# First layer of a three-layer kernel: the transposes of kv move to the bank of kv's sum and ahead of those of q; the second step of the unit loop gets an order of its own

## The chip, the cores and the metric

One Trainium2 chip, one of its cores. The metric is the device time of the program in microseconds (us). The kernel before takes 558.27 us, the median of three runs (557.97 to 558.54). TensorE is called PE here, VectorE DVE, ScalarE ACT, GpSimd POOL, and SP is the engine that issues the DMAs.

## The reference

Three layers follow one another: linear attention, a layer of four attention experts, a layer of eight feed-forward experts. The change is in the first alone. With 4 batches, 8 heads, 576 positions, 64 dimensions and 128 features:

```
def phi(x):                                   # x: q or k, [b, h, s, d]
    proj = x @ w_phi                          # [64, 128]
    proj = proj - max(abs(proj), axis=-1)     # per position
    return concat([exp(proj), exp(-proj)])    # 256 features
q_p, k_p = phi(q), phi(k)
kv  = einsum('bhsf,bhsd->bhfd', k_p, v)
z   = sum(k_p, axis=s)
out = (q_p @ kv) / (q_p . z + 1e-6)
```

The second layer takes out, the third takes the second's result; all of it is fp32.

## The kernel before, in words

The class PhaseA computes the first layer. A unit is one batch and one pair of heads, so there are 16 units. For each unit:

- proj (lines 221 to 243) projects k (512 positions, "k"), q (512 positions, "q") and the last 64 positions of both together ("e"). For k and q two PSUM tiles, one for each head (pjk, pjq), hold the product; DVE takes the largest absolute value (mxk, line 241) and subtracts it (uk, line 242).
- feat_k (line 245) takes the exponentials of uk and ue with both signs on ACT into a_kp, of which there is one buffer (lines 251 and 252), and POOL sums them towards z (zs, lines 255 to 257).
- feat_q (line 259) transposes uq on PE, one head at a time (tile tr, line 268), and ACT takes the exponentials into qp (line 270).
- kv (line 272) accumulates kv on PE in a PSUM tile Y (line 279, 20 rows of the profile for a unit); keys (line 282) adds the sums z to the same tile (line 288), and ACT copies it to kvt (line 291).
- kvtrans (line 293) transposes ue of one unit (line 301) and kvt of the unit before it (line 306) on PE into one PSUM tile, also called kvt in the profile. ACT copies kvt's part to kvs (line 307) and takes exponentials of ue's part into the last 64 columns of qp (line 311).
- num (line 313) and den (line 330) multiply qp by kvs: the tiles pn and, every second unit, pd.

PSUM has eight banks. The pool of the first layer gives five of them to the tags X and tr together (class Banks, and ps.same = {"tr": ("X", 5), "X": ("X", 5)}), two to mm (pje, pn, pd) and one to Y. A unit takes seven tiles of the five: pjk twice, pjq twice, tr twice, and kvtrans' tile. A tile's first matmul waits until the last reader of the bank's earlier tile is done.

run (line 379) goes over 18 steps i: it projects unit i, makes features, kv and z of unit i-1, and num and den of unit i-2. The order of what each step emits is the string A_STEPS: "k0 e0 q0" are projections, "t" gives work of the later layers its turn, "f0", "f1" are feat_q by head, "x0" is kvtrans, "kv0" to "kv3" the sum, "n0 n1" num, "z0" feat_k, "s0" keys, "d0 d1" den. A scheduler then orders what is ready on each engine; each engine runs its list strictly in order. Constants (an identity matrix, counters and the like) are made by make_consts before all this, in part on DVE.

```
A_STEPS = ("k0 e0 q0 t f0 x0 t f1 t a kv0 kv1 A t kv2 kv3 t n0 n1 z0 a t t A s0 d0 d1 t")
pt = self.ps.tile([128, 512], F32, tag="X", name=f"kvt_{i}_{j}")                # kvtrans
r["Y"] = ps.tile([128, 512], F32, tag="Y", name=f"Y_{i}", bufs=1)               # feat_q, h == 0
```

Of the kernel before, what the change touches and what calls it, by code (L numbers as in the profile page):

```python
# [20 lines left out]
NF = 128  # L21
# [11 lines left out]

A_STEPS = ("k0 e0 q0 t f0 x0 t f1 t a kv0 kv1 A t kv2 kv3 t n0 n1 z0 a t t A s0 d0 d1 t")

# [105 lines left out]
def make_consts(ctx, tc, E1=4, E2=8):  # L145
    nc = tc.nc
    cp = ctx.enter_context(tc.tile_pool(name="consts", bufs=1))
    k = Consts()
    one = cp.tile([128, 128], F32, name="ones")
    make_identity(nc, one)  # L150
    eye = cp.tile([128, 128], F32R, name="ident")
    nc.vector.tensor_copy(eye, one)
    k.ident = rd(eye)
    k.identb = cp.tile([128, 128], BF16, name="identb")
    nc.vector.tensor_copy(k.identb, k.ident)
    k.mask = cp.tile([128, 128], BF16, name="cmask")
# [12 lines left out]
    nc.vector.tensor_copy(k.iota, ii)
    k.iota1 = cp.tile([128, 8], F32, name="iota1")  # L170
    nc.vector.tensor_scalar(k.iota1, k.iota, 1.0, None, op0=OP.add)

    k.lower = cp.tile([128, 4, 4], F32, name="lower")
    nc.vector.tensor_tensor(k.lower, k.iota[:, None, 0:4].to_broadcast([128, 4, 4]),
                            k.iota[:, 0:4, None].to_broadcast([128, 4, 4]), op=OP.is_lt)
    return k


class PhaseA:


    def __init__(self, ctx, tc, k, ps, gk, dr, hl, kq, v, w_phi, x1_tile, bg):
        nc = tc.nc
        self.gk, self.dr, self.hl = gk, dr, hl
        self.nc, self.k, self.kq, self.v, self.bg, self.x1_tile = nc, k, kq, v, bg, x1_tile
        self.p2 = ctx.enter_context(tc.tile_pool(name="a_2", bufs=2))
        self.p3 = ctx.enter_context(tc.tile_pool(name="a_3", bufs=2))
        self.p1 = ctx.enter_context(tc.tile_pool(name="a_1", bufs=2))
        self.ps = ps
        self.w_phi = self.p3.tile([128, NF], F32, name="a_w", bufs=1)  # L190
        self.w_in = w_phi
        self.vts = []
# [28 lines left out]
    def proj(self, i, nm):  # L221


        nc, r = self.nc, self.st[i]
        w, raws = self.w_phi, r["raw"]
        n = 1 if nm == "e" else 4
        u = r["u" + nm] = self.p3.tile([128, n, 256], F32, tag=f"u{nm}", name=f"u{nm}_{i}")
        mx = self.p3.tile([128, 2, n], F32, tag=f"mx{nm}", name=f"mx{nm}_{i}")
        if n == 1:
            pt = [self.ps.tile([128, HALF], F32, tag="mm", name=f"pj{nm}_{i}_{h}") for h in range(2)]  # L230
        else:
            pt = [self.ps.tile([128, 512], F32, tag="X", name=f"pj{nm}_{i}_{h}") for h in range(2)]
        for t in range(n):
            for h in range(2):
                p = slice(64 * h, 64 * h + 64)
                c = dict(k=0, e=512, q=640)[nm] + 128 * t
                nc.tensor.matmul(pt[h][:, 128 * t:128 * t + 128], raws[p, c:c + 128], w[p], start=True, stop=True)  # L237
        for h in range(2):
            src = pt[h][:, 0:128 * n].rearrange("p (t f) -> p t f", f=NF)
            m = mx[:, h]  # L240
            nc.vector.tensor_reduce(m, src, axis=AX.X, op=OP.max, apply_absolute_value=True)  # L241
            self.bg.anchor(nc.vector.tensor_tensor(u[:, :, NF * h:NF * h + NF], src,  # L242
                                                   m[:, :, None].to_broadcast([128, n, NF]), op=OP.subtract))

    def feat_k(self, i):
        nc, r = self.nc, self.st[i]
        u, e = r["uk"], r["ue"]
        kp = self.kp
        zs = r["zs"] = self.p3.tile([128, 2, 2, 256], F32, tag="zs", name=f"zs_{i}", bufs=1)
        for sg, sc in ((0, 1.0), (1, -1.0)):  # L250
            nc.scalar.activation(kp[:, 0:4, sg, :], u[:, 0:4, :], AF.Exp, scale=sc)  # L251
            self.bg.anchor(nc.scalar.activation(kp[0:64, 4, sg, :], e[0:64, 0, :], AF.Exp, scale=sc))

            add = nc.gpsimd.tensor_tensor
            add(zs[:, :, sg, :], kp[:, 0:2, sg, :], kp[:, 2:4, sg, :], op=OP.add)  # L255
            add(zs[0:64, 0, sg, :], zs[0:64, 0, sg, :], kp[0:64, 4, sg, :], op=OP.add)
            add(zs[:, 0, sg, :], zs[:, 0, sg, :], zs[:, 1, sg, :], op=OP.add)

    def feat_q(self, i, h):
        nc, r, ps, k = self.nc, self.st[i], self.ps, self.k  # L260
        u = r["uq"]
        if h == 0:
            r["qp"] = self.p1.tile([128, 2, 2, S], F32, tag="qp", name=f"qp_{i}", bufs=3)
            r["Y"] = ps.tile([128, 512], F32, tag="Y", name=f"Y_{i}", bufs=1)
        qp = r["qp"]
        tp = ps.tile([128, 512], F32, tag="tr", name=f"tr_{i}_{h}")
        for t in range(4):
# [4 lines left out]
    def kv(self, i, n):  # L272

        nc, r, k = self.nc, self.st[i], self.k
        Y = r["Y"]
        vt, kp = r["v"], self.kp
        for t in ((0, 1), (2,), (3,), (4,))[n]:
            for h in range(2):
                nc.tensor.matmul(Y[64 * h:64 * h + 64, 0:256], vt[:, t, h, :],  # L279
                                 kp[:, t, :, h * NF:(h + 1) * NF], start=t == 0, stop=t == 4)  # L280

    def keys(self, i):
        nc, r, k = self.nc, self.st[i], self.k
# [95 lines left out]
    def run(self, batch_done, after):  # L379
# [5 lines left out]
        for i in range(n + 2):  # L385
# [1346 lines left out]
```

## Time and profile before

| | us |
|---|---|
| median of three runs | 558.27 |
| the profiled execution | 558.66 |
| its span in the profile | 556.9 |
| PE busy | 530.4 (95%) |
| DVE busy | 364.8 (66%) |
| ACT busy | 264.8 (48%) |
| POOL busy | 148.3 (27%) |

The profiled execution is 1.76 us longer than its span, which is time around the first and the last instruction. Times in rows are counted from the span's start. The first layer takes about the first 180 us, in which work of the second layer is mixed in from about 85 us on. Matmul records are pipelined, so that their durations overlap; a distance from one start to the next is the better measure of what a group costs.

### The profile page before, as it was taken

Reading aid. Unit: us, or ns where it says so; the run is one execution under the profiler, and the core shown is the slowest. Engines: PE = TensorE matmul, PEld = TensorE weight load, DVE = VectorE, ACT = ScalarE, POOL = GpSimd, SP = SyncE. Lnnn points to the kernel's source line nnn. Section 1 sums busy time; section 2 is a strip of 40 time slices with the busy share of each in tenths; the row PEclk is TensorE's granted clock in tenths of the full one; section 3 lists DMA queues with packets and bytes.
Section 4 is the critical chain, followed back from the end, with each engine's and each line's share of the span. In section 5 each row is a group of like instructions: output and inputs, shape, how many; then the busy total and the mean of one; then the engine's idle time right before and its main releaser. Section 6 shows DMA issues by size and latency. Waiting matters only on the chain.

```text
span 556.9 us, 11719 instructions
## 1 busy us (share of the span) xinstructions
PE 530.4 (95%) x4456; PEld 440.7 (79%) x4456; DVE 364.8 (66%) x970; ACT 264.8 (48%) x601; POOL 148.3 (27%) x212
## 2 busy tenths in 40 slices
PE   7999999899999999998999999999999999999995
PEld 6666665566666597767767798999999999999995
DVE  5776677986772777878897776863656274717440
ACT  2857465574474466857656553530434044305200
POOL 5563594368537232020244400000000000000000
PEclk9999999999999999999999999999999999999999
DMA  8323263444105221700200420254435133623011
GB/s 246 124 76 119 79 229 105 123 145 160 61 5 153 96 69 47 254 16 1 78 1 1 140 88 2 77 180 150 144 114 193 46 124 114 234 88 124 2 45 47
DMA packets 32707, 57.05 MB, mean 102 GB/s; under 512 B 7012, under 2 KB 17636, under 8 KB 31620
## 3 DMA queue, kind: packets, MB, share of 16 engines
q1 hardware_dynamic: 32644, 56.24, 31.0%
q8 instruction: 37, 0.61, 0.4%
q14 instruction: 26, 0.21, 0.1%
HBM read 41.86 MB, written 14.36 MB: 101 GB/s over the span
## 4 chain that ended last, share of the span: by engine, by line
PE 75%; DVE 16%; ACT 3%; issue 2%; DMA 2%; SPq 0%; POOL 0%; DVEq 0%; ACTq 0%
PE po_c L63 6%; PE po_c L64 6%; PE po_c L65 6%; PE Y L279 6%; PE ph_c L63 5%; PE ph_c L65 5%; PE ph_c L64 5%; PE pn L323 5%; PE pq_s L702 4%; PE pd L340 3%; PE py_s L848 3%; PE pjk L237 3%; DVE mxk L241 3%; DVE uk L242 2%; PE pt_s L821 2%
## 5 line engine op out<-in xcount | busy, mean ns | idle before, releaser
L63 PE MATMUL ph_c<-xh_c,w1h_c 128*128 128x288 f32 x256 | 76.8, 301 | 0.0
L63 PE MATMUL po_c<-h_c,w2h_c 128*128 128x288 f32 x256 | 76.3, 298 | 0.0
L1415 ACT ACTIVATE h_c<-ph_c 128x288 fp32r<-128x288 f32 x64 | 26.0, 409 | 105.1 <-PE ph_c L65 104.8
L64 PE MATMUL ph_c<-xl_c,w1h_c 128*128 128x288 f32 x256 | 75.8, 296 | 0.0
L64 PE MATMUL po_c<-h_c,w2h_c 128*128 128x288 f32 x256 | 75.6, 295 | 0.0
L65 PE MATMUL ph_c<-xh_c,w1l_c 128*128 128x288 f32 x256 | 75.6, 296 | 0.0
L65 PE MATMUL po_c<-h_c,w2l_c 128*128 128x288 f32 x256 | 75.5, 295 | 0.0
L255 POOL TENSOR_TENSOR zs<-a_kp 128x512 f32<-128x512 f32 x32 | 42.2, 1336 | 69.2 <-PE Y L288 42.7
L270 ACT ACTIVATE qp<-tr 128x512 f32<-128x512 f32 x64 | 35.1, 610 | 50.2 <-PE tr L268 50.2
L1416 DVE SCALAR_TENSOR_TENSOR h_c<-ph_c,h_c 128x288 fp32r<-128x288 f32 x64 | 28.9, 454 | 33.8 <-ACT h_c L1415 33.2
L63 PEld LDWEIGHTS ph_c<-xh_c,w1h_c 128*128 128x128 f32 x256 | 48.1, 188 | 1.7 <-issue 0.9
L63 PEld LDWEIGHTS po_c<-h_c,w2h_c 128*128 128x128 f32 x256 | 48.2, 188 | 0.9 <-issue 0.9
L65 PEld LDWEIGHTS ph_c<-xh_c,w1l_c 128*128 128x128 f32 x256 | 48.1, 188 | 0.5 <-issue 0.5
L64 PEld LDWEIGHTS ph_c<-xl_c,w1h_c 128*128 128x128 f32 x256 | 48.2, 188 | 0.0
L65 PEld LDWEIGHTS po_c<-h_c,w2l_c 128*128 128x128 f32 x256 | 48.2, 188 | 0.0
L64 PEld LDWEIGHTS po_c<-h_c,w2h_c 128*128 128x128 f32 x256 | 48.1, 188 | 0.0
L702 PE MATMUL pq_s<-xh_b,w_s 128*128 128x288 f32 x192 | 43.5, 305 | 1.7 <-DVE q_s L670 1.7
L1438 DVE TENSOR_TENSOR fo_c<-po_c,pb 128x288 f32<-128x288 f32 x32 | 14.5, 455 | 44.5 <-PE po_c L65 44.5
L279 PE MATMUL Y<-a_kp,a_v 128*64 128x256 f32 x320 | 41.1, 386 | 0.0
L251 ACT ACTIVATE a_kp<-uk 128x1024 f32<-128x1024 f32 x32 | 33.6, 1052 | 13.0 <-DVE uk L242 6.4
L323 PE MATMUL pn<-qp,kvs 128*64 128x288 f32 x256 | 36.1, 408 | 0.0
L702 PEld LDWEIGHTS pq_s<-xh_b,w_s 128*128 128x128 f32 x192 | 31.9, 188 | 4.1 <-issue 2.3
(314 smaller groups left out, 1218.9 us busy)
## 6 DMA issues: line engine op xcount, KB each, us to landing
w1raw_c<-in_w_dram SPq DMA_DIRECT2D x16, 512.0 KB, 4.2
w2raw_c<-in_w_dram SPq DMA_DIRECT2D x16, 512.0 KB, 4.4
raw<-in_kq_dram SPq DMA_DIRECT2D x15, 320.0 KB, 3.1
rb<-d SPq DMA_DIRECT2D x32, 144.0 KB, 3.2
x1d<-x SPq DMA_DIRECT2D x4, 1152.0 KB
x2d<-x SPq DMA_DIRECT2D x4, 1152.0 KB
raw<-in_kq_dram SPq DMA_DIRECT2D x16, 256.0 KB, 3.3
a_v<-in_v_dram SPq DMA_DIRECT2D x16, 256.0 KB, 4.2
```

The costliest lines, as they stand in the source:

```text
L63: nc.tensor.matmul(out, lh, rh, start=start, stop=False, **kw)
L64: nc.tensor.matmul(out, lh, rl, start=False, stop=False, **kw)
L65: return nc.tensor.matmul(out, ll, rh, start=False, stop=stop, **kw)
L237: nc.tensor.matmul(pt[h][:, 128 * t:128 * t + 128], raws[p, c:c + 128], w[p], start=True, stop=True)
L251: nc.scalar.activation(kp[:, 0:4, sg, :], u[:, 0:4, :], AF.Exp, scale=sc)
L255: add(zs[:, :, sg, :], kp[:, 0:2, sg, :], kp[:, 2:4, sg, :], op=OP.add)
L270: self.bg.anchor(nc.scalar.activation(qp[:, h, sg, 0:512], tp, AF.Exp, scale=sc))
L279: nc.tensor.matmul(Y[64 * h:64 * h + 64, 0:256], vt[:, t, h, :], kp[:, t, :, h * NF:(h + 1) * NF], start=t == 0, stop=t == 4)
L323: nc.tensor.matmul(pn[64 * h:64 * h + 64, :], kvs[:, sg, 64 * h:64 * h + 64], qp[:, h, sg, c], start=sg == 0, stop=sg == 1)
L702: self.nc.tensor.matmul(out, self.wqkv[t][:, wj, ch, 0:m], x[:, ch, c], start=wj == ch == 0 and x is xh, stop=wj == 1 and ch == 3)
L1415: nc.scalar.activation(hh[:, c], ph, AF.Relu),
L1416: nc.vector.scalar_tensor_tensor(hl[:, c], ph, 0.0, rd(hh[:, c]), op0=OP.max, op1=OP.subtract))
```

## The change

Three things are edited, all in the first layer.

- kvtrans takes its tile from the tag Y (one bank) and no longer from X, and A_STEPS has x0 ahead of f0. The tiles qp and Y are now allocated in kvtrans and kv.
- Step i = 1 has its own order, A_STEPS_1: behind the second unit's k come x0 and the whole kv of the first unit, and only then the second unit's e and q; its matmuls are told to be issued behind the last matmul of that kv.
- In the beginning, each pair "largest value, difference" of the first unit, and of the second unit's k, is issued behind the one before it, the first behind the last constant; and the exponentials of the first unit's k are taken by head, four of 512 columns for two of 1024.

```diff
-A_STEPS = ("k0 e0 q0 t f0 x0 t f1 t a kv0 kv1 A t kv2 kv3 t n0 n1 z0 a t t A s0 d0 d1 t")
+A_STEPS = ("k0 e0 q0 t x0 f0 t f1 t a kv0 kv1 A t kv2 kv3 t n0 n1 z0 a t t A s0 d0 d1 t")
+A_STEPS_1 = ("k0 t x0 kv0 kv1 t kv2 kv3 e0 q0 t f0 t f1 t z0 t t s0 t")
...
+                with ExitStack() as x:
+                    if i == 1 and nm != "k":
+                        x.enter_context(after(self.kv_last.ins))
+                    nc.tensor.matmul(pt[h][:, 128 * t:128 * t + 128], raws[p, c:c + 128], w[p], start=True, stop=True)
...
+            with ExitStack() as x:
+                if i == 0 or i == 1 and nm == "k":
+                    x.enter_context(after(self.last.ins))
+                nc.vector.tensor_reduce(m, src, axis=AX.X, op=OP.max, apply_absolute_value=True)
+            last = nc.vector.tensor_tensor(u[:, :, NF * h:NF * h + NF], src,
+                                           m[:, :, None].to_broadcast([128, n, NF]), op=OP.subtract)
+            self.last = last
...
+        if not i:
+            for h in range(2):
+                for sg, sc in ((0, 1.0), (1, -1.0)):
+                    c = slice(h * NF, (h + 1) * NF)
+                    nc.scalar.activation(kp[:, 0:4, sg, c], u[:, 0:4, c], AF.Exp, scale=sc)
...
-        if h == 0:
-            r["qp"] = self.p1.tile([128, 2, 2, S], F32, tag="qp", name=f"qp_{i}", bufs=3)
-            r["Y"] = ps.tile([128, 512], F32, tag="Y", name=f"Y_{i}", bufs=1)
...
+        if n == 0:
+            r["Y"] = self.ps.tile([128, 512], F32, tag="Y", name=f"Y_{i}", bufs=1)
...
-        pt = self.ps.tile([128, 512], F32, tag="X", name=f"kvt_{i}_{j}")
+        pt = self.ps.tile([128, 512], F32, tag="Y", name=f"kvt_{i}_{j}", bufs=1)
         if j >= 0:
             r = self.st[j]
+            r["qp"] = self.p1.tile([128, 2, 2, S], F32, tag="qp", name=f"qp_{j}", bufs=3)
...
-            for step in A_STEPS.split():
+            for step in (A_STEPS_1 if i == 1 else A_STEPS).split():
```

First place: PE in the middle of a usual step, before. tr_0 and tr_1 are q's transposes by head, kvt_2 kvtrans' tile, Y the sum; in brackets stands what a row waits for.

```order
L268 MATMUL tr_0_471<-ident,uq_339 128x128 x4
L301 MATMUL kvt_2_478<-ident,ue_329 128x128 [waits DVE_49,PE_49]
L301 MATMUL kvt_2_478<-ident,ue_329 128x128
L306 MATMUL kvt_2_478<-ident,kvt_420 128x128 [waits Activation_49]
L306 MATMUL kvt_2_478<-ident,kvt_420 128x128 x2
L268 MATMUL tr_1_488<-ident,uq_339 128x128 [waits DVE_49,PE_49]
L268 MATMUL tr_1_488<-ident,uq_339 128x128 x3
L279 MATMUL Y_470<-a_kp,a_v_139 64x256 [waits DMAHW0_49]
L279 MATMUL Y_470<-a_kp,a_v_139 64x256 x7
```

The same step of the changed kernel on PE:

```order
L317 MATMUL kvt_2_471<-ident,ue_331 128x128 [waits Activation_49]
L317 MATMUL kvt_2_471<-ident,ue_331 128x128
L322 MATMUL kvt_2_471<-ident,kvt_422 128x128 x3
L281 MATMUL tr_0_482<-ident,uq_341 128x128 x4
L281 MATMUL tr_1_489<-ident,uq_341 128x128 [waits DVE_49,PE_49]
L281 MATMUL tr_1_489<-ident,uq_341 128x128 x3
L294 MATMUL Y_496<-a_kp,a_v_139 64x256 [waits DMAHW0_49,PE_49,Activation_49]
L294 MATMUL Y_496<-a_kp,a_v_139 64x256 x7
```

kvt now stands first and waits for ACT alone; the second head's transposes still wait for DVE; and Y's first matmul waits for ACT as well.

Second place: ACT in the first two units, before (uk_158 and ue_174 are the first unit's, uk_218 and ue_234 the second's).

```order
L251 ACTIVATE a_kp<-uk_158 128x4x256 x2
L252 ACTIVATE a_kp<-ue_174 64x256 x2
L270 ACTIVATE qp_260<-tr_0_262 128x512 x2
L311 ACTIVATE qp_260<-kvt_-1_0_269 128x2x64 x2
L251 ACTIVATE a_kp<-uk_218 128x4x256
L270 ACTIVATE qp_260<-tr_1_274 128x512 x2
L252 ACTIVATE a_kp<-ue_234 64x256
L251 ACTIVATE a_kp<-uk_218 128x4x256
L252 ACTIVATE a_kp<-ue_234 64x256
L291 ACTIVATE kvt_306<-Y_261 128x384
```

The same of the changed kernel (there uk_220 and ue_253 are the second unit's):

```order
L264 ACTIVATE a_kp<-uk_158 128x4x128 x4
L268 ACTIVATE a_kp<-ue_174 64x256 x2
L327 ACTIVATE qp_237<-kvt_-1_0_236 128x2x64 x2
L267 ACTIVATE a_kp<-uk_220 128x4x256 x2
L283 ACTIVATE qp_237<-tr_0_279 128x512 x2
L283 ACTIVATE qp_237<-tr_1_286 128x512 x2
L268 ACTIVATE a_kp<-ue_253 64x256 x2
L306 ACTIVATE kvt_308<-Y_242 128x384
```

Both exponentials of the second unit's k now stand ahead of all those of the first unit's q, and the copy of Y stays behind them.

Third place: DVE in the beginning, before, from the first projection to the first difference of e.

```order
L241 TENSOR_REDUCE mxk_159<-pjk_0_160 128x4
L241 TENSOR_REDUCE mxk_159<-pjk_1_161 128x4
L242 TENSOR_TENSOR uk_158<-pjk_0_160,mxk_159 128x4x128
L242 TENSOR_TENSOR uk_158<-pjk_1_161,mxk_159 128x4x128
L169 CAST iota<-iota_i 128x8
L241 TENSOR_REDUCE mxe_175<-pje_0_176 128x1
L152 CAST ident<-ones 128x128
L163 CAST cmaskr<-cmask 128x64
L171 TENSOR_SCALAR iota_79<-iota 128x8
L155 CAST identb<-ident 128x128
L165 MEMSET ones 128x128
```

The same of the changed kernel, from the last constants on:

```order
L166 MEMSET ones 128x128
L175 TENSOR_TENSOR lower<-iota 128x16
L1027 COPY b_ex<-iota 128x8
L249 TENSOR_REDUCE mxk_159<-pjk_0_160 128x4
L250 TENSOR_TENSOR uk_158<-pjk_0_160,mxk_159 128x4x128
L249 TENSOR_REDUCE mxk_159<-pjk_1_161 128x4
L250 TENSOR_TENSOR uk_158<-pjk_1_161,mxk_159 128x4x128
L249 TENSOR_REDUCE mxe_175<-pje_0_176 128x1
L250 TENSOR_TENSOR ue_174<-pje_0_176,mxe_175 128x128
```

All constants come ahead of the first projection's values, and each difference stands right behind its own largest value.

## Rows read from the trace of the kernel before

**Rows 1.** The page, the chain that ended last, shares of the span by engine.
```profile
PE 75%; DVE 16%; ACT 3%; issue 2%; DMA 2%; SPq 0%; POOL 0%; DVEq 0%; ACTq 0%
```
**Rows 2.** Waits of PE, 0 to 180 us: total us, times, longest.
```profile
PE kvt L301 <- DVE uk L242: 4.6, 11, 1.0
```
**Rows 3.** Timeline of a usual unit: start us, us, instruction, idle before.
```profile
39.95 0.66 PE L268 MATMUL tr<-ident,uq 128*128 128x128 f32 x4
40.14 1.28 DVE L242 TENSOR_TENSOR uk<-pjk,mxk 128x512 f32<-128x512 f32 x2
...
40.96 0.41 PE L301 MATMUL kvt<-ident,ue 128*128 128x128 f32 x2 [0.36 <-DVE uk L242]
...
41.21 0.49 PE L306 MATMUL kvt<-ident,kvt 128*128 128x128 f32 x3
...
41.56 0.63 PE L268 MATMUL tr<-ident,uq 128*128 128x128 f32 x4
...
41.74 0.49 ACT L307 ACTIVATE kvs<-kvt 128x384 f32<-128x384 f32 x1
...
42.12 2.38 PE L279 MATMUL Y<-a_kp,a_v 128*64 128x256 f32 x20
42.12 0.44 ACT L311 ACTIVATE qp<-kvt 128x128 f32<-128x128 f32 x2
...
46.73 1.16 PE L237 MATMUL pjk<-a_w,raw 64*128 64x128 f32 x16
```
**Rows 4.** Timeline of the first 27 us.
```profile
5.87 1.29 DVE L241 TENSOR_REDUCE mxk<-pjk 128x4 f32<-128x512 f32 x2 [4.94 <-PE pjk L237]
...
9.42 0.28 DVE L241 TENSOR_REDUCE mxe<-pje 128x1 f32<-128x128 f32 x1
...
15.40 0.46 ACT L311 ACTIVATE qp<-kvt_-1_0_269 128x128 f32<-128x128 f32 x2
...
15.72 1.08 ACT L251 ACTIVATE a_kp<-uk 128x1024 f32<-128x1024 f32 x1
...
15.98 0.66 PE L268 MATMUL tr<-ident,uq 128*128 128x128 f32 x4
...
16.68 1.10 ACT L270 ACTIVATE qp<-tr 128x512 f32<-128x512 f32 x2
...
17.65 0.41 ACT L252 ACTIVATE a_kp<-ue 64x256 f32<-64x256 f32 x1
...
17.95 1.05 ACT L251 ACTIVATE a_kp<-uk 128x1024 f32<-128x1024 f32 x1
...
19.21 0.47 ACT L291 ACTIVATE kvt<-Y 128x384 f32<-128x384 f32 x1
...
26.58 1.16 PE L237 MATMUL pjk<-a_w,raw 64*128 64x128 f32 x16
```
**Rows 5.** Timeline of DVE, a difference right behind its own largest value.
```profile
95.55 0.67 DVE L241 TENSOR_REDUCE mxq<-pjq 128x4 f32<-128x512 f32 x1
96.25 0.69 DVE L242 TENSOR_TENSOR uq<-pjq,mxq 128x512 f32<-128x512 f32 x1
```
**Rows 6.** Timeline of PE, the units whose wait is not the usual one.
```profile
118.96 0.41 PE L301 MATMUL kvt<-ident,ue 128*128 128x128 f32 x2 [0.48 <-DVE uk L242]
129.74 0.41 PE L301 MATMUL kvt<-ident,ue 128*128 128x128 f32 x2 [0.16 <-DVE uk L242]
139.92 0.63 PE L268 MATMUL tr<-ident,uq 128*128 128x128 f32 x4 [0.36 <-DVE uk L242]
```
**Rows 7.** Busy us by stretch: length, PE, PEld, DVE, ACT, POOL, clock, DMA.
```profile
100.00:120.00 20.00, 18.32 (x185) 12.09 (x184) 19.00 (x50) 11.28 (x24) 9.26 (x10) 1.00 0.43 127
```
**Rows 8.** Timeline of POOL and DVE near 90 us.
```profile
89.05 2.55 POOL L255 TENSOR_TENSOR zs<-a_kp 128x512 f32<-128x512 f32 x2 [4.53 <-PE Y L288]
...
90.28 1.36 DVE L483 TENSOR_TENSOR w<-L,mx 128x20 f32<-128x20 f32 x1
```
**Rows 9.** Line 483, 80 to 300 us: duration ns min/median/max.
```profile
L483 DVE TENSOR_TENSOR w<-L,mx x4: 171/172/1360, 90.3 to 250.2; 128x20 f32<-128x20 f32 x4
```

More of the change, by code (lines that the diff above doesn't have):

```diff
@@ L173, in make_consts @@
     k.lower = cp.tile([128, 4, 4], F32, name="lower")
-    nc.vector.tensor_tensor(k.lower, k.iota[:, None, 0:4].to_broadcast([128, 4, 4]),
-                            k.iota[:, 0:4, None].to_broadcast([128, 4, 4]), op=OP.is_lt)
+    k.last = nc.vector.tensor_tensor(k.lower, k.iota[:, None, 0:4].to_broadcast([128, 4, 4]),
+                                     k.iota[:, 0:4, None].to_broadcast([128, 4, 4]), op=OP.is_lt)
     return k
@@ L199, in __init__ @@
         nc.gpsimd.memset(self.kp[64:128, 4], 0.0)
+        self.last = k.last
         self.st = {}
@@ L221, in proj @@
     def proj(self, i, nm):
-        nc, r = self.nc, self.st[i]
+        nc, r, after = self.nc, self.st[i], self.bg.tc.issue_after
         w, raws = self.w_phi, r["raw"]
@@ L236, in proj @@
                 c = dict(k=0, e=512, q=640)[nm] + 128 * t
-                nc.tensor.matmul(pt[h][:, 128 * t:128 * t + 128], raws[p, c:c + 128], w[p], start=True, stop=True)
+                with ExitStack() as x:
+                    if i == 1 and nm != "k":
+                        x.enter_context(after(self.kv_last.ins))
+                    nc.tensor.matmul(pt[h][:, 128 * t:128 * t + 128], raws[p, c:c + 128], w[p], start=True, stop=True)
         for h in range(2):
@@ L240, in proj @@
             m = mx[:, h]
-            nc.vector.tensor_reduce(m, src, axis=AX.X, op=OP.max, apply_absolute_value=True)
-            self.bg.anchor(nc.vector.tensor_tensor(u[:, :, NF * h:NF * h + NF], src,
-                                                   m[:, :, None].to_broadcast([128, n, NF]), op=OP.subtract))
+            with ExitStack() as x:
[5 more added lines that the diff above has]
+            self.last = last
+            self.bg.anchor(last)
     def feat_k(self, i):
@@ L249, in feat_k @@
         zs = r["zs"] = self.p3.tile([128, 2, 2, 256], F32, tag="zs", name=f"zs_{i}", bufs=1)
+        if not i:
[3 more added lines that the diff above has]
+                    nc.scalar.activation(kp[:, 0:4, sg, c], u[:, 0:4, c], AF.Exp, scale=sc)
         for sg, sc in ((0, 1.0), (1, -1.0)):
-            nc.scalar.activation(kp[:, 0:4, sg, :], u[:, 0:4, :], AF.Exp, scale=sc)
+            if i:
+                nc.scalar.activation(kp[:, 0:4, sg, :], u[:, 0:4, :], AF.Exp, scale=sc)
             self.bg.anchor(nc.scalar.activation(kp[0:64, 4, sg, :], e[0:64, 0, :], AF.Exp, scale=sc))
@@ L278, in kv @@
             for h in range(2):
-                nc.tensor.matmul(Y[64 * h:64 * h + 64, 0:256], vt[:, t, h, :],
-                                 kp[:, t, :, h * NF:(h + 1) * NF], start=t == 0, stop=t == 4)
+                self.kv_last = nc.tensor.matmul(Y[64 * h:64 * h + 64, 0:256], vt[:, t, h, :],
+                                                kp[:, t, :, h * NF:(h + 1) * NF], start=t == 0, stop=t == 4)
     def keys(self, i):
```

## The prediction

> **What bounds the kernel now.** I read the page first, then PE's waits over the first layer, then the timeline of one usual unit, then that of the first 27 us, and last the stretch in which the second layer's gate is computed beside the first. The chain that ended last runs on PE for 75% of the span and on DVE for 16% [rows 1], so time is won where PE waits, and where DVE is the chain. In the first 180 us one wait of PE comes back: line 301 waits for the difference uk, 11 times, 4.6 us in all [rows 2].
>
> The timeline of a usual unit shows what this wait is. q's first transposes start at 39.95; then PE stands idle for 0.36 us until DVE has written uk's first half, and goes on with kvtrans at 40.96 [rows 3]. The data has nothing to do with uk: kvtrans transposes ue and kvt, both of units before. It is the bank. A unit takes seven tiles of five banks, and the sixth, kvtrans', falls on that of the same unit's pjk, which DVE still reads. The Trainium skill says the same of such a picture (Perfetto Trace Analysis, Optimization Strategy: a gap that comes back at the same place on the engine that should be busy can mean too few buffers in PSUM); the sum doesn't rest on it.
>
> **The change, usual units.** Measured from start to start, kvtrans takes 41.56 − 40.96 = 0.60 us, four transposes of q 42.12 − 41.56 = 0.56, and from Y's start to the next unit's k it is 46.73 − 42.12 = 4.61 [rows 3]. Before, from q's first transposes to Y it is 42.12 − 39.95 = 2.17. After, kvtrans is first, with a bank that ACT has left long before, and six tiles remain for the five banks, so the one that meets pjk's bank is q's second transposes. 0.60 + 0.56 + 0.56 = 1.72, so 0.45 are to be had (the 0.36 of idle time, and the pipeline's running empty). Two waits can eat of it:
>
> - The second transposes of q wait for uk's first half. It lands at 40.14 + 0.68 = 40.82 (half of 1.28 and an overlap of 0.08), PE went on 0.14 behind that; after the change they would be due at 39.95 + 0.60 + 0.56 = 41.11 [rows 3]. Nothing to wait for.
> - Y now shares its bank with kvtrans' tile, so its first matmul waits until ACT has read that tile: the copy to kvs, and two exponentials. ACT's copy starts 41.74 − 40.96 = 0.78 behind kvtrans' start, and the last exponential ends at 42.12 + 0.44 = 42.56, 1.60 behind it [rows 3]. PE starts behind such a release at 15.98, where the exponentials ended at 15.40 + 0.46 = 15.86: 0.12 more [rows 4]. That makes 1.72, exactly when PE is through with its 1.72 of transposes. So there is no cover left: whatever ACT is late, Y is late.
>
> What stands behind Y on PE is num, keys and the next unit's k, so a late Y delays all. The bounds of a usual unit: 0.45 if ACT keeps these times, and 0.15 if the three reads don't overlap as they do here (an estimate: 0.49 and twice some 0.30, 0.30 us longer). I take 0.40, near the upper end, because the times of ACT are rows of these very instructions. Eight units are usual: six up to 82 us and two near 153 and 162 us; of the 4.6 us, less the long one and the two below, each has (4.6 − 1.0 − 0.48 − 0.16) / 8 = 0.37 [rows 2, 6], as the one shown. 8 × 0.40 = 3.2 us.
>
> **The other units.** At 93.58, the longest of the 11, DVE is the bound and not PE: DVE is busy for 19.00 of 20 us between 100 and 120 us [rows 7], and PE's waits there give nothing. At 118.96 [rows 6] PE had put six matmuls of Y ahead of the wait, which now come behind it, 6 × 0.12 = 0.7 us (2.38 us for 20 [rows 3]) against 0.60 for kvtrans, which moves ahead: 0. At 129.74 the wait is 0.16 [rows 6], so 0.2. At 139.92 q's transposes themselves wait [rows 6], since the gate's transposes take a bank too; kvtrans now fills that gap: 0.4, with 0 as the other end, for Y then waits for ACT in a busier place. Together 0.6.
>
> **The beginning.** Here the chain is DVE and then ACT. Constants go where DVE waited for the first k (4.94 us idle before 5.87 [rows 4]), so they cost nothing. But each difference now stands right behind its own largest value, and 95.55 to 96.25 shows the price of that: 0.70 from start to start [rows 5], for 0.60 where another instruction stands between. DVE after the change: first unit's k, from 5.87 [rows 4], 0.70 + 0.60 + 0.70 + 0.60 = 2.6, to 8.47; four short ones of e (0.28 each [rows 4], an estimate of 0.25 apart), to 9.47; q 2.6, to 12.07; the second unit's k with one short one between, 0.70 + 0.60 + 0.60 + 0.20 + 0.68, to 14.85.
>
> ACT has the first unit's exponentials done, and the first Y ends, well before this: uk's first head is there at 7.25; four exponentials of 0.54 with a gap between the heads end near 9.7, e's and kvtrans' at some 10.7, and 20 matmuls of 0.12 end near 13.2. So the four exponentials for two, and the early Y, are covered by 1.6 us, and become the chain only if these take that much longer. From 14.85 on ACT is the chain, in its new order: two exponentials of uk, 2 × 0.96 (15.72 to 16.68); two pairs for q, 2 × 0.97 (16.68 to 17.65); two of ue, 2 × 0.30 (17.65 to 17.95); the copy of Y, 0.47 [rows 4]. With 0.03 for the first start that is 19.81, and PE starts the third step's kvtrans at 19.93. With 1.72 to Y and 4.61 to the next k it is 26.26, where before it is 26.58 [rows 4]: 0.3 us won. Most of what the early Y gives is lost again at ACT, where the copy of Y stands behind eight other instructions. The bounds: 1.3, if the copy is not held up and PE goes on without a stop (the third unit's q needs banks that DVE leaves, with three short ones and 2.6 for the second unit's q behind 14.77, near 18.1, so PE is through with the projections near 19.0, an estimate, 0.9 to 1.0 before 19.93), and −0.5, if DVE's chain comes out 0.8 longer.
>
> SP issues one pair of loads of v ahead of two of k and q instead of behind; both are for units more than 10 us off, so nothing.
>
> **What the DVE stretch does.** It begins behind PE's work near 89 us, so it starts earlier by all that was won until then, and the rest of the kernel hangs on the first layer's results. But its length is not fixed. At 90.28 a subtraction of 20 columns takes 1.36 us, until POOL's sum of 89.05 + 2.55 = 91.60 is done [rows 8]; the same instruction takes 0.17 elsewhere [rows 9]. The Trainium skill has this (SBUF — State Buffer, Who interferes with whom): DVE and POOL share a port pair, which one holds for a whole instruction. The trace agrees: the subtraction ends 0.04 behind POOL's sum. After the change Y of that unit, the exponentials and POOL's sums behind them come up to 0.6 us earlier against DVE's list, so other small instructions will meet them. One meeting more or less with a long sum is 1.36 − 0.17 = 1.2 us either way. I take 0.
>
> **The sum.** 3.2 + 0.6 + 0.3 = 4.1 us. The profiled execution of 558.66 would become 554.56; it lies 0.39 above the median of 558.27, so the median becomes 554.2.
>
> **Rivals.**
> 1. ACT's release becomes the wait: the three reads take 0.30 longer than above. For it: they have no cover at all. Against it: they overlap in the rows. Then a usual unit gives 0.15: 8 × 0.15 = 1.2, others 0.3, beginning 0.3: 1.8, and 556.5. The Trainium skill speaks for this side (PSUM — Partial Sum Buffer, Summary: rules for kernel authors: what is read while matmuls run belongs in another bank than they write); here the two are serialised by the wait.
> 2. The stretch near 90 to 119 us meets one or two more long sums of POOL: 4.1 − 1.2 or − 2.4, so 555.4 to 556.6. For it: the meetings are many there. Against: as many may go.
> 3. The wait only moves, to q's second transposes or to Y, in all units: the beginning alone is left, 558.0. Against: 41.11 is 0.15 behind the moment at which uk is read.
> 4. Slower: Y's first matmul is released by ACT more than 2.17 us behind kvtrans' start, because ACT takes the copy only when other work ahead of it in its list is done. Each unit then loses; at 2.57, say, 0.4 in each of 11 units: 4.4 slower less 0.3, so 562.4. Against it: ACT is free when the tile is ready, for its own list has q's exponentials behind the copy now. It decides from 0.45 us of lateness on.
>
> **How the numbers follow.** The forecast, with its mixture of small ends, 62%; rival 1 15%, rival 2 10%, rival 3 7%, rival 4 6%. The range: the lower end is the forecast with the upper bounds of units and beginning, 8 × 0.05 + 1.0, and some of the DVE stretch: 552.4. The upper end takes in rivals 1 and 2: 556.8. A measurement of this kernel can tell 0.2%, some 1.1 us, from no change. Slower by over that: rival 4, 6%. Within: rival 3 and a little, 8%. Faster: the rest, 86%.
>
> **What will show it.** In the profile after, PE's wait of line 317 (kvtrans) for uk is gone in the usual units, and from kvtrans' start to Y's it is 1.7 to 1.8 us; a longer way, with ACT as the releaser, is rival 1. From the first transposes behind a usual unit's projections to the next unit's k, without den, it is 6.3 to 6.4 us, for 46.73 − 39.95 = 6.78 [rows 3]. The fourth unit's k starts near 26.3, with PE idle about 1 us before the third step's kvtrans and ACT as what it waited for. The small instructions of the gate between 90 and 119 us tell rival 2. The forecast is wrong if the median is above 556.8, and its main step if kvtrans still waits, or Y does for more than 0.2 us.

## The result, and the profile after

The changed kernel takes 553.08 us (median of 4 runs, 552.15 to 553.90) beside 558.40 for the kernel before (4 runs): a ratio of 0.9904, 95% interval 0.9885 to 0.9922. Two later sets, each beside its own runs of before, gave 0.9915 (0.9890 to 0.9939) and 0.9923 (0.9904 to 0.9941). The forecast was 554.2, the range 552.4 to 556.8: the time lies in it, 1.1 us below the forecast. The profiled execution took 553.34 us, with a span of 551.5.

The chain that ended last, from the page of the changed kernel, for [rows 1]: DVE's share has gone from 16% to 11%, and PE has it.

```profile
PE 79%; DVE 11%; ACT 4%; DMA 3%; issue 1%; POOL 0%; SPq 0%; DVEq 0%; ACTq 0%; POOLq 0%
```

PE's waits in the first 180 us, for [rows 2] (total us, times, longest):

```profile
PE pc L516 <- DVE cnt L513: 2.2, 1, 2.2
PE kvt L317 <- ACT kvt L306: 0.8, 1, 0.8
...
PE Y L294 <- ACT qp L327: 0.5, 1, 0.5
PE tr L281 <- DVE uk L250: 0.5, 1, 0.5
```

kvtrans' eleven waits for uk are gone. One wait for uk is left, at q's second transposes at 90.28, and one of Y for ACT, at the first Y (11.12). Apart from the wait for the first load, the largest that is left is a single one for the gate's count, cnt. It was 1.4 us in the kernel before, and it comes back below.

A usual unit, for [rows 3] (start us, us, instruction, idle before):

```profile
36.88 1.16 PE L242 MATMUL pjk<-a_w,raw 64*128 64x128 f32 x16
...
39.09 0.44 PE L317 MATMUL kvt<-ident,ue 128*128 128x128 f32 x2
39.37 0.49 PE L322 MATMUL kvt<-ident,kvt 128*128 128x128 f32 x3
39.70 1.04 PE L281 MATMUL tr<-ident,uq 128*128 128x128 f32 x8
39.90 0.49 ACT L323 ACTIVATE kvs<-kvt 128x384 f32<-128x384 f32 x1 [4.46 <-PE kvt L322]
40.28 0.44 ACT L327 ACTIVATE qp<-kvt 128x128 f32<-128x128 f32 x2
...
40.77 1.93 PEld L294 LDWEIGHTS Y<-a_kp,a_v 128*64 128x64 f32 x20 [0.28 <-ACT qp L327]
40.78 2.38 PE L294 MATMUL Y<-a_kp,a_v 128*64 128x256 f32 x20
...
45.38 1.16 PE L242 MATMUL pjk<-a_w,raw 64*128 64x128 f32 x16
```

From kvtrans to Y it is 40.78 − 39.09 = 1.69 us, where from q's first transposes it was 2.17; k to k it is 8.50 us. ACT ends its last read of kvtrans' tile at 40.28 + 0.44 = 40.72, and the transposes end at 39.70 + 1.04 = 40.74. Y's weights do wait for ACT (0.28 us), more than the 0.2 us that the prediction set as a sign that its main step is wrong. But PE is at the transposes until 40.74, so that Y's first matmul hardly waits: the two paths meet within 0.02 us.

The beginning, for [rows 4]:

```profile
5.68 0.69 DVE L249 TENSOR_REDUCE mxk<-pjk 128x4 f32<-128x512 f32 x1 [2.11 <-PE pjk L242]
...
14.16 0.68 DVE L250 TENSOR_TENSOR uk<-pjk,mxk 128x512 f32<-128x512 f32 x1
...
14.96 2.00 ACT L267 ACTIVATE a_kp<-uk 128x1024 f32<-128x1024 f32 x2 [3.89 <-PE pjq L242]
16.88 2.04 ACT L283 ACTIVATE qp<-tr 128x512 f32<-128x512 f32 x4
...
19.39 0.48 ACT L306 ACTIVATE kvt<-Y 128x384 f32<-128x384 f32 x1
...
19.93 0.44 PE L317 MATMUL kvt<-ident,ue 128*128 128x128 f32 x2 [0.76 <-ACT kvt L306]
...
26.21 1.16 PE L242 MATMUL pjk<-a_w,raw 64*128 64x128 f32 x16
```

kvtrans of the third step starts at 19.93, as forecast to the hundredth, and the fourth unit's k at 26.21 for a forecast of 26.26. The hundredth is luck: DVE began 0.19 us earlier than in the kernel before (5.68 for 5.87), and took 0.18 longer to the end of the second unit's uk (14.84 − 5.68 = 9.16, for 8.98 in the forecast).

Where the time came from: the start of the same instruction in the two traces, and what the stretch up to it won, in us:

| stretch, instruction at its end | before | after | won, forecast | won, measured |
|---|---|---|---|---|
| beginning, fourth unit's k | 26.58 | 26.21 | 0.3 | 0.37 |
| six usual units, Y | 82.41 | 79.11 | 2.4 | 2.93 |
| gate's stretch, sums of keys | 112.99 | 109.83 | 0 | −0.14 |
| unit with the wait at 118.96, sums of keys | 123.87 | 119.66 | 0 | 1.05 |
| unit with the wait at 129.74, sums of keys | 135.14 | 130.33 | 0.2 | 0.60 |
| unit with the wait at 139.92, sums of keys | 147.29 | 142.49 | 0.4 | −0.01 |
| two usual units, sums of keys | 167.53 | 161.76 | 0.8 | 0.97 |
| the rest, end of the span | 556.9 | 551.5 | 0 | −0.4 |

The sum is 5.4 of the span, for 4.1 forecast. Rows above their forecast give 2.2 us more than it, rows below it 0.95 less, so that the sum is nearer to the forecast than its terms are.

### The profile page after: what moved, and what is told of

Its sections match the earlier page's. It is cut to its first block, busy times and chain, and to the rows that moved or that the text cites. A ratio compares the mean times of both kernels' runs of the same rounds, so it can differ in the third digit from the quotient of the medians.

```text
span 551.5 us, 11691 instructions
## 1 busy us (share of the span) xinstructions
PE 526.8 (96%) x4456; PEld 440.6 (80%) x4456; DVE 366.3 (66%) x970; ACT 263.8 (48%) x603; POOL 148.2 (27%) x212
## 4 chain that ended last, share of the span: by engine, by line
PE 79%; DVE 11%; ACT 4%; DMA 3%; issue 1%; POOL 0%; SPq 0%; DVEq 0%; ACTq 0%; POOLq 0%
PE po_c L64 6%; PE po_c L65 6%; PE po_c L66 6%; PE Y L294 6%; PE pn L339 5%; PE pq_s L718 5%; PE ph_c L64 5%; PE ph_c L66 5%; PE ph_c L65 5%; PE pd L356 3%; PE py_s L864 3%; PE pjk L242 3%; PE pjq L242 2%; PE pt_s L837 2%; PE pg L455 2%; PE tr L281 2%
## 5 line engine op out<-in xcount | busy, mean ns | idle before, releaser
L294 PE MATMUL Y<-a_kp,a_v 128*64 128x256 f32 x320 | 39.2, 385 | 1.0 <-ACT qp L327 0.5
L267 ACT ACTIVATE a_kp<-uk 128x1024 f32<-128x1024 f32 x30 | 31.5, 1052 | 6.8 <-PE pjq L242 3.9
L283 ACT ACTIVATE qp<-tr 128x512 f32<-128x512 f32 x64 | 33.6, 634 | 1.3 <-PE tr L281 1.3
```

What stands on the lines that cost most here:

```text
L283: self.bg.anchor(nc.scalar.activation(qp[:, h, sg, 0:512], tp, AF.Exp, scale=sc))
L294: self.kv_last = nc.tensor.matmul(Y[64 * h:64 * h + 64, 0:256], vt[:, t, h, :], kp[:, t, :, h * NF:(h + 1) * NF], start=t == 0, stop=t == 4)
```

## The experiments

The questions, in order: which part of the change gives the time (usual units or beginning), whether bank or order does it, what the edits of the beginning are worth one by one, and what happens behind the wait for cnt.

**e1_usual**: the kernel before with the usual units' part alone.

```diff
-A_STEPS = ("k0 e0 q0 t f0 x0 t f1 t a kv0 kv1 A t kv2 kv3 t n0 n1 z0 a t t A s0 d0 d1 t")
+A_STEPS = ("k0 e0 q0 t x0 f0 t f1 t a kv0 kv1 A t kv2 kv3 t n0 n1 z0 a t t A s0 d0 d1 t")
...
-        pt = self.ps.tile([128, 512], F32, tag="X", name=f"kvt_{i}_{j}")
+        pt = self.ps.tile([128, 512], F32, tag="Y", name=f"kvt_{i}_{j}", bufs=1)
```

> The bank and the order of the usual unit alone: kvtrans' tile in Y's bank and kvtrans ahead of q's transposes; constants, early first Y, and split exponentials of the beginning as before. Theory (the gain comes from the usual units, the beginning gives only what moved the fourth unit's k, 26.58 to 26.21): 553.1 + 0.4 = 553.5 us, and a unit of 8.50 us as in the changed kernel. Rival (the two parts help each other, because Y's bank is free for kvtrans only if the beginning is in the new order, or because the gate's stretch meets other sums of POOL when it starts 0.4 us later): 554.5 or more.

Measured: 552.47 us (4 runs), ratio 0.9894 (0.9879 to 0.9910). The whole gain is there without any edit of the beginning. Its timeline (DVE's first largest value, the fourth unit's k):

```profile
6.33 1.29 DVE L241 TENSOR_REDUCE mxk<-pjk 128x4 f32<-128x512 f32 x2 [5.40 <-PE pjk L237]
...
26.21 1.16 PE L237 MATMUL pjk<-a_w,raw 64*128 64x128 f32 x16
```

The first loads landed later in this execution, and still the fourth unit's k starts at 26.21, the same as in the changed kernel. From the first largest value it is 19.88 us; it is 20.53 in the changed kernel and 26.58 − 5.87 = 20.71 before [rows 4]. So the 0.37 us that the beginning shows belong to the bank and the order, which hold for the third step too. The distance from the first largest value is itself not steady between executions: the two of e9 below, of one kernel, differ by 0.68. The units behind it start within 0.04 us of those of the changed kernel up to 170 us.

**e2_order**: the order of e1_usual without the bank (the first pair of lines of its diff; qp and Y are allocated as in e1_usual).

> The order alone: kvtrans ahead of q's transposes, its tile still among the five banks. Then it takes the fifth bank, and q's two transposes fall on the two banks of pjk. Theory (the bank is the wait, not the order): kvtrans from 39.95 to 40.55 for a unit as in the kernel before, q's first transposes wait for uk's first half until 40.96, its second for uk's second half until 41.42 + 0.14 = 41.56, and Y starts at 42.12 as before: 0 to 0.05 us a unit, 557.9 to 558.4 us. Rival (kvtrans ahead of q gives the gain by itself, since it fills the time in which PE stood): 0.3 or more a unit, 555 us or less.

Measured: 557.73 us, ratio 0.9993 (0.9984 to 1.0002): nothing. PE's waits in its first 180 us show where the wait went:

```profile
PE tr L265 <- DVE uk L242: 3.2, 10, 0.9
```

kvtrans is through early, and q's transposes now wait for the same uk. A unit is as long as before (Y to Y 51.94 − 42.96 = 8.98). The order by itself moves the wait; it does not take it away.

**e3_bank**: the bank of e1_usual without the order (the second pair of lines).

> The bank alone: kvtrans' tile in Y's bank, but q's first transposes ahead of it as before. Then ACT has q's two first exponentials ahead of the three reads of kvtrans' tile. Theory (Y is released by ACT's reads and has no cover): PE is through with its transposes at 39.95 + 1.72 = 41.67 in the unit of the kernel before, ACT with q's two exponentials at some 41.7 and with the three reads behind them near 42.6, so Y can start only near 42.75, 0.6 later than before; a few of the next unit's pjk go ahead of Y and fill 0.3 to 0.5 of that: 0.1 to 0.3 a unit lost, 559 to 562 us. Rival (the bank of uk was the whole matter, and ACT's reads are covered by Y's weights and the next projections): 553.5 to 555 us.

Measured: 557.28 us, ratio 0.9981 (0.9972 to 0.9990). A usual unit of its timeline:

```profile
40.02 0.66 PE L267 MATMUL tr<-ident,uq 128*128 128x128 f32 x4
40.51 0.38 PE L302 MATMUL kvt<-ident,ue 128*128 128x128 f32 x2
...
41.05 0.60 PE L267 MATMUL tr<-ident,uq 128*128 128x128 f32 x4
41.58 0.75 PE L237 MATMUL pjk<-a_w,raw 64*128 64x128 f32 x6
42.27 0.70 PE L324 MATMUL pn<-qp,kvs 128*64 128x288 f32 x2
42.58 2.55 PE L280 MATMUL Y<-a_kp,a_v 128*64 128x256 f32 x20
```

and ACT beside it:

```profile
40.71 1.08 ACT L269 ACTIVATE qp<-tr 128x512 f32<-128x512 f32 x2 [3.70 <-PE tr L267]
41.68 0.50 ACT L308 ACTIVATE kvs<-kvt 128x384 f32<-128x384 f32 x1
42.05 0.47 ACT L312 ACTIVATE qp<-kvt 128x128 f32<-128x128 f32 x2
```

For the unit the theory held: ACT has q's exponentials first, its last read of kvtrans' tile ends at 42.05 + 0.47 = 42.52, and Y starts 0.06 behind that. Pieces of k and pn ahead of Y fill the time, and a unit takes 9.13 us, Y to Y, for 8.99 before: 0.14 lost, within the 0.1 to 0.3 expected. So Y does hang on ACT's reads, and it is the order that takes ACT off the path. For the whole kernel the expectation of 559 to 562 was wrong. What the units lose (sums of keys at 76.17 for 75.50) is made up where the second layer's work sets in (the next ones at 88.42 in both), and stays so to the sums of keys at 123.77 for 123.87. PE's wait for cnt is 0.6 us for 1.4. The median's 1.1 us lie behind this: in the trace the unit at 139.92 takes 0.95 us less (146.28 − 135.08 for 147.29 − 135.14), and what follows the first layer some 1.5 less. Why, no run shows.

**e4_begin**: the changed kernel with the usual units' part undone, so the edits of the beginning alone (the diff is the reverse of that of e1_usual, but that step 1 keeps its own order).

> The beginning alone: constants first, each difference behind its own largest value, split exponentials, the first Y and the second unit's kvtrans in the new order; the usual units as before. Theory: the fourth unit's k near 26.2 to 26.5 for 26.58, and from there on the units of before: 558.0 us (557.7 to 558.4). Rival (the early start moves the gate's stretch to other sums of POOL, and much of the 5.3 us came from there): 556.5 us or less.

Measured: 558.13 us, ratio 1.0006 (0.9991 to 1.0021). The fourth unit's k starts at 26.80, 21.08 us behind the first largest value at 5.72: later than before, not earlier.

**after_again** and **after_third**: the changed kernel, unedited.

> The changed kernel once more, beside the three others of this set. e1_usual, which has the usual units' part alone, came out at 552.47 us, 0.6 below the 553.08 of the changed kernel, and both reach the fourth unit's k at 26.21 us. Theory (the edits of the beginning cost time: measured from DVE's first largest value the fourth unit's k comes 20.53 us later in the changed kernel, 19.88 later in e1_usual, whose first loads landed 0.6 us later in the profiled execution): 553.1 us again. Rival (0.6 us is the scatter between sets of runs): 552.5 us.

> The changed kernel once more, as the neighbour of the three others. In the profiled executions PE waits 2.15 to 2.18 us for the count cnt near 94.4 us (1.4 in the kernel before); behind that wait the granted clock was 1.00 in the first profile and 0.53 to 0.62 between 96 and 100 us in the second, where the matmuls pn took 3.56 us for 2.16. Theory (the longer idle time sometimes lets the clock fall, and costs 0.6 us or more then): 553.1 to 553.9 us, with either picture in the profile.

Measured: 553.87 us, 0.9915 (0.9890 to 0.9939), and 554.18, 0.9923 (0.9904 to 0.9941), in two sets; the fourth unit's k 20.52 and 20.51 us behind the first largest value, so that 0.65 to the one trace of e1_usual stays. Whether that shows in the time can't be told: the intervals overlap with that of e1_usual. What the first of these traces shows near 96 us is new (timeline of PE):

```profile
96.50 0.59 PE L516 MATMUL pc<-cnt,ones 128*128 128x4 f32 x2 [2.15 <-DVE cnt L513]
97.02 3.56 PE L339 MATMUL pn<-qp,kvs 128*64 128x288 f32 x16
```

The same in the first trace of the changed kernel:

```profile
96.62 0.39 PE L516 MATMUL pc<-cnt,ones 128*128 128x4 f32 x2 [2.18 <-DVE cnt L513]
96.94 2.16 PE L339 MATMUL pn<-qp,kvs 128*64 128x288 f32 x16
```

Sixteen matmuls take 3.56 us for 2.16. The windows of after_again say why (length, busy us of PE, PEld, DVE, ACT, POOL, then the granted clock, DMA share, GB/s):

```profile
94.00:96.00 2.00, 0.35 (x8) 0.15 (x4) 1.90 (x4) 2.00 (x5) 1.92 (x2) 1.00 0.49 146
96.00:98.00 2.00, 1.50 (x6) 1.03 (x8) 1.86 (x7) 0.35 (x1) 1.92 (x3) 0.62 0.03 8
98.00:100.00 2.00, 2.00 (x12) 1.02 (x10) 1.97 (x10) 0.74 (x2) 1.54 (x3) 0.53 0.00 0
100.00:102.00 2.00, 2.00 (x32) 0.89 (x32) 0.96 (x5) 0.24 (x1) 0.00 (x0) 1.00 0.05 5
```

The granted clock falls to half (1.2 of 2.4 GHz) at the end of PE's wait for cnt, and is back near 100 us. In windows of 0.25 us it falls at 96.5 here; in the four others in which it fell, between 0.5 us before the end of the wait and 1.2 us behind it. From Y to the next Y it is 15.49 us in this execution, 14.75 and 14.73 in the two of the changed kernel in which the clock stayed at 1.00.

**e5_no_early_y**: the changed kernel without the early first Y.

```diff
-            for step in (A_STEPS_1 if i == 1 else A_STEPS).split():
+            for step in A_STEPS.split():
...
-                    if i == 1 and nm != "k":
-                        x.enter_context(after(self.kv_last.ins))
```

> The changed kernel without the early first Y: the second unit's kvtrans in the usual order, constants first, differences right behind their largest values and the split exponentials kept. Theory (what costs is the early Y: ACT waits 3.89 us for uk of the second unit, and has eight instructions between it and the copy of Y): from DVE's first largest value to the fourth unit's k 19.9 us or less, 552.5 us or less. Rival (what costs is the chain of dependent pairs on DVE, 0.1 us each): 20.5 us, 553.1 us.

Measured: 552.97 us, 0.9900 (0.9879 to 0.9920). The fourth unit's k at 26.23, 20.10 us behind the first largest value at 6.13: between theory (19.9) and rival (20.5), nearer to the theory. By this one trace two thirds of the 0.65 are the early Y, and the rest is left for the chain of pairs and the split exponentials.

**e7_copy_early**: the changed kernel with the copy of Y earlier in ACT's list.

```diff
-A_STEPS_1 = ("k0 t x0 kv0 kv1 t kv2 kv3 e0 q0 t f0 t f1 t z0 t t s0 t")
+A_STEPS_1 = ("k0 t x0 kv0 kv1 t kv2 kv3 e0 q0 t s0 t f0 t f1 t z0 t t")
```

> The changed kernel with the first unit's sums of keys and the copy of Y right behind q, so that ACT takes the copy behind two instructions and not behind eight. Theory (the early Y was lost at ACT's list): copy at 16.9 instead of 19.39, kvtrans of the third step near 19.1 to 19.2, when PE is through with the projections, instead of 19.93, ACT's copy of kvs near 20.2, Y near 21.0 instead of 21.61: 0.6 us less than the changed kernel beside it. Rival (the third unit's projections, which need banks that DVE leaves, or POOL's sums hold it): 0.2 us or less.

Measured: 553.74 us, 0.9911 (0.9890 to 0.9933), no difference from the changed kernel beside it. The mechanism held: the copy is at 16.84 for 19.39, kvtrans at 19.43, the fourth unit's k at 25.72, 0.47 us earlier from the first largest value than in the changed kernel (0.6 expected). It is 0.5 us ahead at the Y near 90 us, and then loses it: the clock is at 0.50 from 96 to 102 us, and Y to Y takes 17.04 us.

**e9_consts** and **e9_again**: e1_usual with the constants alone ahead on DVE (k.last is the last of them).

```diff
+            with ExitStack() as x:
+                if i == 0:
+                    x.enter_context(self.bg.tc.issue_after(k.last.ins))
+                nc.vector.tensor_reduce(m, src, axis=AX.X, op=OP.max, apply_absolute_value=True)
```

> e1_usual with one edit of the beginning: DVE's eight constants ahead of its first largest value instead of between the first unit's uk and ue. In e1_usual they take from 8.73 to 9.68 there, on DVE's way to the second unit's uk, and ACT's unbroken chain to the copy of Y starts behind q's transposes, which wait for that uk. Theory (the constants were the one part of the beginning that is worth something): all behind them 0.9 us earlier, 19.0 us from DVE's first largest value to the fourth unit's k for 19.88, 551.6 us. Rival (something else holds ACT or PE there): 19.9 us, 552.4 us.

> e9_consts once more: in its first profile the fourth unit's k starts at 24.89 us, 1.3 earlier than in the changed kernel, but the clock was 0.53 to 0.61 from 96 to 100 us, and only 0.5 of the 1.3 was left at the next Y. Theory: 0.5 to 1.3 us faster than the changed kernel beside it, 552.0 to 552.6 us where that has 553.1; where the profile shows the clock at 1.00 behind the wait for cnt, a span near 549.6 us, where not, near 550.4. Rival (the gate's stretch gives all of it back whatever the clock): no difference.

Measured: 553.70 us, 0.9916 (0.9892 to 0.9941), and 553.92, 0.9924 (0.9908 to 0.9941). The timeline of the first:

```profile
5.51 1.29 DVE L244 TENSOR_REDUCE mxk<-pjk 128x4 f32<-128x512 f32 x2 [1.94 <-PE pjk L237]
...
24.89 1.16 PE L237 MATMUL pjk<-a_w,raw 64*128 64x128 f32 x16
```

19.38 us from the first largest value to the fourth unit's k, 0.50 less than in e1_usual (0.9 expected). In e9_again it is 20.06, 0.18 more than in e1_usual; there thirteen matmuls of pjk from 8.57 on took 2.29 us, where in the first thirteen from 7.44 on took 1.41. In the first, PE is 1.3 us ahead of the changed kernel at 24.89 and at the Y at 89.51. At the next Y, 105.06, 0.5 is left, with the clock at half again behind the wait for cnt; in e9_again the clock fell for longer, and Y to Y took 16.92 us. No difference in the time, against the theory.

**e10_pc_late** (on e9_consts) and **e11_after_pc_late** (on the changed kernel): the matmul that waits for cnt is told two ticks later (two later yields are taken out, so that what follows keeps its tick).

```diff
-        yield 2
+        yield 4
         pc = ps.tile([128, HALF], F32, tag="mm", name=f"pc_{b}")
...
         nc.vector.tensor_tensor(w, w, sm[:, :, None].to_broadcast([128, QT, 4]), op=OP.mult)
-        yield
...
-        yield
```

> e9_consts with the matmul pc, which waits for cnt, told two ticks later, so that the matmuls pn (2.16 us) and one of the keys' sums stand ahead of it on PE instead of the keys' sums and twelve of the next unit's k (1.3 us). Theory (the wait for cnt costs twice, as idle time and by the clock behind it): the wait shrinks from 2.2 to some 1.3 us, the clock stays at 1.00 from 94 to 104 us, and the stretch from one Y to the next takes 14.0 us for 15.55: 1 to 1.5 us faster than e9_again where that shows the clock fallen, 0.7 where not; near 551.3 us. Rival (DVE bounds the stretch, and takes the copy of pn now ahead of the gate's list): 0 to 0.4 us slower than e9_again.

> The same edit of pc in the changed kernel itself, without that of the constants. Theory: the wait for cnt shrinks from 2.2 to some 1.3 us, as short as in the kernel before, the clock stays at 1.00 from 94 to 104 us, and the stretch from Y near 90.8 to the next near 105.6 takes 14.0 us for 14.75 (clock full) or 15.5 (clock fallen): 0.7 to 1.5 us faster than the changed kernel beside it. Rival (DVE bounds the stretch): 0 to 0.4 us slower.

Measured: 553.28 us, 0.9905 (0.9883 to 0.9928), and 554.26, 0.9928 (0.9913 to 0.9944): no difference that can be told from e9_again and after_third beside them. PE in e10_pc_late:

```profile
94.23 0.38 PE L503 MATMUL pc<-cnt,ones 128*128 128x4 f32 x2
...
97.45 0.94 PE L237 MATMUL pjk<-a_w,raw 64*128 64x128 f32 x12
101.33 0.94 PE L237 MATMUL pje<-a_w,raw 64*128 64x128 f32 x3 [2.94 <-DVE dn L345]
...
102.13 2.06 PE L237 MATMUL pjq<-a_w,raw 64*128 64x128 f32 x15
```

The wait for cnt is gone, and a longer one stands 7 us behind it: 2.94 us for DVE, which is 2.95 in e11_after_pc_late. Behind it the clock is at half, and Y to Y takes 17.56 and 17.57 us. The theory failed: DVE bounds this stretch, and what PE doesn't wait for at one place it waits for at the next. Part of that is POOL, as in [rows 8]. A row of DVE's between tot and dn in e10_pc_late:

```profile
98.34 2.18 DVE L518 TENSOR_TENSOR c<-w,hot 128x80 f32<-128x80 f32 x1
```

The same instruction takes 0.23 us at its other places; here it ends 0.10 behind POOL's sums (99.03 + 1.39 = 100.42). In e11_after_pc_late it takes 2.19.

## Why the prediction was right, and where it wasn't

**Usual units.** The mechanism was right in every part. The bank was the wait (e2_order), ACT's reads are what Y hangs on (e3_bank, where Y starts 0.06 us behind them), and the wait for uk is gone. Only the size was off: 0.40 was taken for a unit, 0.45 was the upper end, and 0.49 was measured. Rival 1 took nothing; the release cost 0.06 us and not the 0.12 that I had read at another place, and it is 1.69 from kvtrans to Y, not 1.72. Eight units at 0.49 are 0.7 us more than the sum had. There is no cover left, as the prediction said, so a slower read on ACT would show in every unit.

**The unit at 118.96.** The step "six matmuls of Y come behind the wait, 0.7 us against 0.60 for kvtrans: 0" is wrong. The trace of before, beside the row in [rows 6]:

```profile
116.82 0.66 PE L268 MATMUL tr<-ident,uq 128*128 128x128 f32 x4
117.40 1.08 PE L279 MATMUL Y<-a_kp,a_v 128*64 128x256 f32 x6
...
120.06 1.73 PE L279 MATMUL Y<-a_kp,a_v 128*64 128x256 f32 x13
```

From Y's first six to kvtrans it is 118.96 − 117.40 = 1.56 us, of which six matmuls are 0.7: 0.86 us stood empty, though the idle column says 0.48, since the modelled end of the last matmul counts as busy there. kvtrans' own 0.60 is no price, as it is done in either order. The changed kernel:

```profile
113.73 0.44 PE L317 MATMUL kvt<-ident,ue 128*128 128x128 f32 x2
...
115.41 2.38 PE L294 MATMUL Y<-a_kp,a_v 128*64 128x256 f32 x20
```

1.68 us to Y, and 1.05 us won in the unit. For the one at 129.74 the same column misled: 128.92 to 130.89 was 1.97 from q's transposes to Y, with 0.16 in the column [rows 6], and it is 1.68 after; the other 0.3 is k's matmuls, no longer split around den.

**The unit at 139.92.** 0.4 was forecast, with 0 as the other end "for Y then waits for ACT in a busier place". It was 0, in part for that reason: at 136.31 PE waits 0.32 us for ACT's exponentials of kvtrans' tile (the row that waits is pn, which stands ahead of Y there). q's second transposes stand in the middle of Y in both kernels (137.78; 143.01 before), and now some 0.5 us of PE stand empty ahead of them, for 0.1 before. What holds them is not shown.

**The beginning.** Its times were right (kvtrans 19.93, k 26.21 for 26.26), its cause was not. I derived 0.3 from the new orders on DVE and ACT, and compared with a kernel that lacked the bank as well. With the bank and the order and without these edits the fourth unit's k is as early (e1_usual), and with these edits and without bank and order it is 0.2 later than before (e4_begin). The edits together cost some 0.65 us at that point, measured from DVE's first largest value: the early Y most of it (e5_no_early_y), by the list of ACT, as the prediction said (e7_copy_early wins 0.47 by moving one copy). The constants ahead are worth 0.5 in one trace and −0.2 in another (e9_consts, e9_again). All but the three traces of the changed kernel are single ones, so these parts are indications. None of it could be seen in the time.

**The gate's stretch.** I took 0 for it. In the profiled execution it was −0.14, and the meeting of DVE and POOL at 90.28 [rows 8] was still there, at 86.99 with 1.35 us. Rival 2 looked at POOL: no more meetings came than there were. What came was a thing that I had not weighed. PE is 3.9 us earlier at the Y in that stretch (90.83 for 94.73), DVE's list only 3.1 (ri_b, the gate's last result, at 100.22 for 103.31). So PE's wait for cnt grows from 1.4 to 2.2 us, and behind the longer wait the clock falls in some executions. Before:

```profile
97.97 1.30 POOL L255 TENSOR_TENSOR zs<-a_kp 128x512 f32<-128x512 f32 x1 [3.63 <-ACT a_kp L251]
98.11 1.19 DVE L494 TENSOR_SCALAR sel<-sel 128x20 f32<-128x20 f32 x1
...
99.69 0.39 PE L500 MATMUL pc<-cnt,ones 128*128 128x4 f32 x2 [1.36 <-DVE cnt L497]
```

After:

```profile
94.07 1.31 POOL L271 TENSOR_TENSOR zs<-a_kp 128x512 f32<-128x512 f32 x1 [3.03 <-ACT a_kp L267]
94.25 1.22 DVE L506 TENSOR_TENSOR c<-c,c 128x80 f32<-128x80 f32 x1
...
96.38 0.19 DVE L513 TENSOR_REDUCE cnt<-sel 128x4 f32<-128x20 f32 x1
```

These rows show what else is in the wait. Ahead of cnt, DVE's list meets a sum of POOL in both kernels: sel takes 1.19 us for 0.18 elsewhere, c<-c,c 1.22 for 0.24, and they end 0.03 and 0.09 us behind the sum. By the difference that is about 1 us of either wait, an estimate. In e3_bank the sum begins at 98.09 and holds the first instruction behind cnt (0.94 us); there PE's wait is 0.6. Moving that sum of POOL was not tried.

Of the eight profiled executions, of the changed kernel and its variants, with a wait of 2.15 to 2.18 us the clock fell in five; in the four with waits of 0.6 to 1.4 us it was never below 1.00 there; behind 2.94 and 2.95 us it fell in both. The 16 runs of the changed kernel show what this takes, by the mean granted clock of each (which counts a fall anywhere in the program):

```
mean clock of the run   runs   median us
0.997 to 0.999          4      552.66
0.994 to 0.996          7      553.52
0.991 to 0.992          5      555.20
```

Of 49 runs of the kernel before, 41 are at 0.997 or above (median 558.32), eight at 0.994 to 0.996 (558.66), and none is below 0.994. So the change is worth some 5.7 us where the clock holds (558.32 − 552.66), and some 2.5 less where it falls for longest (555.20 − 552.66). That the idle time is the cause is borne out by these counts, not by a run that fills the wait and changes nothing else: the attempt with pc moved the wait instead, and another was not tried.

No version tried beats the changed kernel beyond its interval. e1_usual has its whole gain without the edits of the beginning.

## What to carry to other kernels

When a tile waits for a bank, count the tiles of a round against the banks, and move the one whose data is ready first to a bank that is free, and ahead of those that wait: bank or order alone gave nothing or next to it here. Read what a wait costs from the starts of the instructions around it, less their own work, and not from the idle column. And when one engine gets faster up to a place where another is the bound, look at how long it will stand there, and at what holds that other engine.

## What the runs showed of the hardware

- The granted clock of TensorE fell to half at or near the end of a single wait of 2.2 us in the middle of a busy stretch, in five of eight profiled executions, for some 3 to 7 us; Y to Y took 0.7 to 2.3 us longer then. The Trainium skill (TensorE: Matmul & The Clock Gate, Why this matters for your kernels) warns of idle gaps of PE between bursts of matmuls, but of longer ones than this. Here the runs go further: one gap of 2.2 us, in a kernel whose PE is busy for 96% of the span, was enough, in one execution and not in the next.
- On DVE, a difference right behind its own largest value starts 0.70 to 0.73 us after it (5.68 to 6.41 in the changed kernel), for 0.60 between neighbours that don't depend on one another (11.01 to 11.61 in the kernel before). On ACT, four exponentials of 512 columns took 1.15 us a pair, 2.30 in all, where two of 1024 took 2.00 together.
- Small instructions of DVE that met a sum of POOL took 0.94 to 2.18 us for 0.17 to 0.24, and ended 0.03 to 0.10 us behind it, in the kernel before, the changed kernel, e3_bank and e10_pc_late.
